# Where the output head pairs turn the next head pair, and where they take the left-over queries

## The chip, the cores and the metric

The kernel runs on one core of one Trainium2 chip. The metric is the device time of one execution in microseconds; before the change it is 324.42 us, the median of 3 runs (324.22 to 324.81). A core has a tensor engine for matrix products (TensorE; PE in the profile, PEld for its weight loads), a vector engine (DVE), a scalar engine (ACT), GpSimd (POOL) and a queue engine (SP). Each works through its own list of instructions and waits on semaphores for the others. TensorE writes into PSUM, eight banks of 128 x 512 fp32, from which DVE and ACT read.

## The reference

Attention with a relative position bias, followed by a feed-forward layer whose hidden units are the largest of three products:

```
scores = q @ k^T / sqrt(64) + bias[|i - j|]       # 8 batches, 8 heads, 576 positions, head size 64
attn   = softmax(scores)
x      = (attn @ v), heads side by side           # 4608 tokens x 512
h      = max(x @ w1, x @ w2, x @ w3)              # 4608 x 768
out    = h @ w_out                                # 4608 x 512
```

## The kernel before

Work goes by head pairs: batch `b` and pair `hp`, four pairs to a batch, 32 in all. The 576 positions are four tiles of 128 and a remainder of 64, "left-over" keys and queries. A head pair does these things:

- The queries and keys of the pair are turned by `turn` (L782): 28 small transposes on TensorE (tile `tp`, one buffer of the score pool) and five copies on DVE into `qT`, `kT` and `xT`. `turn(n)`, called in pair `n`, turns the queries and keys of pair `n + 1` and the attention output of pair `n - 2`.
- Scores for one key tile (`key_scores`, L877) are two matmuls and one exponential on ACT into `e4`; the bias is applied afterwards by DVE, as a product with exponentials of the bias (`times_band`, L826, and its kin). Left-over keys (`left_keys_rows`, L906, tile `sct`) and left-over queries (`left_queries`, L934, tile `scq`; then `times_band_left`, L941) go into `el` in the same way.
- Attention times values (`attend_rows`, L994, tile `a`) comes one head pair later: it is the first thing that a pair does for the pair before it, after which DVE divides by the sums.

Between these, each head pair carries one stage of the feed-forward layer of the batch before, handed out as a queue of `stages` (L393 to 666). Three stages of four are gate stages: two feature blocks of `hT` each, for which TensorE computes the first and second product in the pair and the third in the next pair (`after`, L541), and DVE takes the largest. The last maximum is `larger` (L549, instruction L551); in the code it is the callback `largest`. The fourth stage is the output stage (`outputs`, L621): four products of 128 tokens with `w_out`, of which the first two form one tile `ps0` and the third and fourth one tile each by halves (`halves`, L581). Head pairs that carry it are the *output head pairs*: (3,1), (4,1), (5,1), (6,1) and (7,1), five in all. The diff touches the gate stage's `run` too, but only in its list of arguments and one call.

A product over 128 rows is split in two halves of 64 rows that run side by side on TensorE, with a `rows(False)` part and a `rows(True)` part (`pair`, L370). In the output stage `rows0(False, c0, c1)` works on feature blocks `c0` to `c1 - 1`: blocks 0 to 3 were finished in earlier pairs, blocks 4 and 5 are written by the two instructions of `largest` in this same head pair. `begin1` is the first part of the third product, `end0` the second part of `ps0` with the ACT copy of its first half into `osb`; `put` is the DVE copy of its other half, and `end1` the second part and the DVE copy of the third product.

PSUM is full. The score pool `ps_s` has two buffers (of two banks), through which `sc`, `sct`, `tp` and `scq` rotate in the order of their creation; `ps_a` has one buffer, used by `ps0` and `a` in turn; `ps_f` has one, used by the third gate product and the output products by halves.

Order is written out by hand. TensorE's matmuls (`mm`, L108) and transposes (`tr`, L112), DVE's instructions (`dve_copy`, L125, and the rest), ACT's copies and, in this part of the kernel, its exponentials are all kept in program order on their engine; so are the DMA issues on their queues. An instruction that has to wait holds up everything behind it on its engine. The order within an output head pair is the body of `run` (L638), called from the main loop at L1294:

Of the kernel before, what the change touches and what calls it, by code (L numbers as in the profile page):

```python
# [39 lines left out]
def kernel(  # L40
# [19 lines left out]
    HP = H // 2  # L60
# [309 lines left out]
    def pair(n, operands, pool, tag, w=CH):  # L370


        box = []

        def rows(swap, c0=0, c1=n):
            if not swap and c0 == 0:
                box.append(pool().tile([P, 2, CH], F32, tag=tag, name="psp"))
            made = []
            for c in range(c0, c1):
                for par in range(2):  # L380
                    i = par ^ swap
                    lhsT, rhs = operands[i](slice(64 * par, 64 * par + 64), c)
                    made.append(mm(
                        box[0][:, i, 0:w], lhsT=lhsT, rhs=rhs, start=not swap and c == 0, stop=swap and c == n - 1,
                    ))
            if swap:
                behind_rows(made[0], box[1])
            elif c1 == n:
                box.append(first_rows_end())

        return lambda: box[0][:, :, 0:w], rows

    def ffn(t0, nt, last, tiled=False):  # L393
# [124 lines left out]
        def gates(fb, m):  # L518

            def gate(i, ki):  # L520
                return lambda r, c: (
                    w_bf[ki][r, c, (fb + i) * P : (fb + i) * P + P], xT[r, c, t0 : t0 + nt]
                )

            ps0, rows0 = pair(DCH, (gate(0, 0), gate(1, 0)), lambda: ps_a, "a")
            ps1, rows1 = pair(DCH, (gate(0, 1), gate(1, 1)), lambda: ps_f, "ff")

            def end0():
                rows0(True)
                m.append(ffnw.tile([P, 2, CH], BF16, tag="m", name="m"))  # L530
                for i in range(2):
                    st[fb + i]["m"] = m[0][:, i, :]
                act_copy(m[0][:], ps0())

            def end1():
                rows1(True)
                return lambda: inorder(nc.vector.tensor_tensor(  # L537
                    out=m[0][:], in0=ps1(), in1=m[0][:], op=ALU.max,
                ))

            def after():  # L541
                ps2, rows2 = pair(DCH, (gate(0, 2), gate(1, 2)), lambda: ps_f, "ff")

                def end(parts=1):
                    rows2(True)
                    out_ = hT[:, fb * CH : fb * CH + 2 * CH].rearrange("p (i t) -> p i t", i=2)
                    n = 2 // parts

                    def larger():  # L549
                        for i in range(0, 2, n):  # L550
                            inorder(nc.vector.tensor_tensor(  # L551
                                out=out_[:, i : i + n], in0=ps2()[:, i : i + n], in1=m[0][:, i : i + n], op=ALU.max,
                            ))
                    return larger
                return lambda: rows2(False), end

            def run(more_scores, left, ahead, largest, bands, keys):
                rows0(False)
                largest()
                more_scores()  # L560
                bands()
                end0()
                rows1(False)
                left()
                ahead()
                end1()()

            run.keys_late = False
            return run, after

        def columns(j, c0, c1):
# [49 lines left out]
        def outputs():  # L621
            ps0, rows0 = pair(FCH, [columns(j, 0, d_model) for j in range(2)], lambda: ps_a, "a")

            def end0():
                rows0(True)
                osb = osb_tile()
                first = act_copy(osb[:], ps0()[:, 0, :])
                put_later(0, osb)

                def put():  # L630
                    osb = osb_tile()
                    other_banks([dve_copy(osb[:], ps0()[:, 1, :])], [first])
                    put_later(1, osb)
                return put

            begin1, end1 = halves(2)

            def run(more_scores, left, ahead, largest, bands, keys):  # L638
                end_keys = keys()
                rows0(False, 0, 1)  # L640
                end_keys()
                rows0(False, 1, KT)
                largest()
                more_scores()
                bands()
                rows0(False, KT)
                begin1()
                put = end0()
                left()
                ahead()  # L650
                put()
                end1()()

            run.keys_late = True
            return run, lambda: halves(3)
# [221 lines left out]
    def key_scores(qT, kT, e4, t):  # L877
        sc = ps_s.tile([P, 2, QM], F32, tag="sc", name="sc")
        for par in range(2):
            r = slice(64 * par, 64 * par + 64)  # L880
            mm(sc[:, par, :], lhsT=kT[r, P * t : P * t + P], rhs=qT[r, 0:QM])
        exp(e4[:, t], sc[:])
# [230 lines left out]
    for hp in range(HP):  # L1113
        qT, kT = (x[:, hp, :] for x in qk[0])
        e4, el = e_tiles()
# [29 lines left out]
    for hp in range(HP):  # L1145
        qT, kT = (x[:, hp, :] for x in qk[0])
        if begun:
            e4, el = begun.pop()
            more_transposes(hp + 1)
            scores(qT, kT, e4, 1, 2)  # L1150
        else:
            e4, el = e_tiles()
# [58 lines left out]
    for b, hp in [(b, hp) for b in range(1, B) for hp in range(HP)]:  # L1211
        if hp == 0:
            x_sb[b] = x_tile()
        qT, kT = (x[:, hp, :] for x in qk[b])
        e4, el = begun[0] if begun else e_tiles()
# [13 lines left out]
        if tiled:  # L1229
            run, after = stages.pop(0)  # L1230
# [37 lines left out]
        if rows:  # L1268
            begin2, end2 = thirds.pop()()
            if not run.keys_late:  # L1270
                end_keys = left_keys_rows(qT, kT, el)
            begin2()
            if not run.keys_late:
                end_keys()
            if not lead:
                key_scores(qT, kT, e4, 2)
            largest = end2(2 if run.keys_late else 1)

            def bands():
                times_band(hp, e4, 2, 0, QM, inorder)  # L1280
                times_bandt(hp, el)
                times_band(hp, e4, 3, 0, QM, inorder)

            def left():
                left_queries(hp, qT, kT, el)
                times_band_left(hp, el)

            def ahead():
                n = HP * b + hp + 1
                if n < HP * B:  # L1290
                    begun.append(e_tiles())
                    key_scores(*(x[:, n % HP, :] for x in qk[n // HP]), begun[0][0], 0)

            run(  # L1294
                lambda: (turn(HP * b + hp), key_scores(qT, kT, e4, 3)), left, ahead, largest, bands,
                lambda: left_keys_rows(qT, kT, el),
            )
            thirds.append(after)
        elif tiled:
            if len(pending) > 1:  # L1300
                fill(DCH)
            keys()
            fill(FCH)
            times_band(hp, e4, 0, 0, QS, inorder)
            begin0, end0, begin1, end1, alone = run
            scores(qT, kT, e4, *order[2])
            begin0()
            exp_left = left_queries(hp, qT, kT, el)
            turned_1 = begin1()
            if (b, hp) == (3, 0):  # L1310
                left_keys(hp, qT, kT, el, 0, S)
            times_band(hp, e4, 1, 0, QM, inorder)
            band_left = times_bandt(hp, el)
            go_behind([band_left], turned_1[-1])
            times_band_left(hp, el)
            scores(qT, kT, e4, *order[3])
            dve0 = end0([exp_left])
            dve1 = end1([band_left])
            times_band(hp, e4, 2, 0, QM, inorder)
            dve0()  # L1320
            times_band(hp, e4, 3, 0, QM, inorder)
            dve1()
            pending.extend((n, [fn]) for n, fn in alone)
        else:
            fill(8 if (b, hp) == (2, 1) else rate, keys, *([lambda: None] if together else []))
            if b == 1 and hp + 1 < HP:
                spread_packed(hp + 1, nc.vector)
            times_bandt(hp, el)


            def beside_scores():
                banks = [pool.tile([P, KT * 64], F32, tag=tag, name="scq") for pool, tag in ((ps_a, "a"), (ps_f, "ff"))]
                turn_left_queries(qT, kT, banks)
                put_left_queries(el, banks)

            visit(qT, kT, e4, order[2:], None if together else beside_scores, el=el if together else None)
# [100 lines left out]
```

## Time and profile before

| what | value |
|---|---|
| median of 3 runs | 324.42 us (324.22 to 324.81) |
| the profiled execution's own time | 324.71 us |
| its span, first to last instruction | 322.9 us |
| granted TensorE clock, mean | 0.998 |
| TensorE busy | 306.3 us, 95% of the span |
| DVE busy | 235.9 us, 73% |
| ACT busy | 200.8 us, 62% |
| POOL busy | 143.4 us, 44% |
| `psp` products 64x512, count | 800 matmuls, 99.4 us busy |

Times of single instructions are from this one execution. Where two instructions follow each other on one engine, the second can start shortly before the first is shown to end, so sums go from start to start. A line such as L109, L113 or L126 is that of a helper that records all matmuls, transposes or copies; tiles tell them apart. The ends of matmuls are modelled. In lists of waits, a wait for several semaphores is put down to the one that came last.

### The profile page before, as it was taken

The numbers are of one execution on the slowest core, as the hardware profiler recorded it, in microseconds if no ns is written. First come the engines' busy times: TensorE is split into PE (matmuls) and PEld (weight loads), VectorE is DVE, ScalarE is ACT, GpSimd is POOL, SyncE is SP. The second block draws the span as 40 slices with busy tenths as digits, with TensorE's granted clock in tenths as the row PEclk, the third lists the DMA queues.
The fourth block names the chain that finished last, engine by engine and source line by source line (L and its number), as shares of the span: only waits on it lengthen the run. The fifth ranks groups of instructions, "written<-read, shape, count | busy, mean of one in ns | idle before, by whom it ended". The sixth has DMA issues, their size and how long they took to land.

```text
span 322.9 us, 12536 instructions
## 1 busy us (share of the span) xinstructions
PE 306.3 (95%) x5539; PEld 197.5 (61%) x5539; DVE 235.9 (73%) x576; ACT 200.8 (62%) x268; POOL 143.4 (44%) x199
## 2 busy tenths in 40 slices
PE   7789999999999899989999899989998999999995
PEld 2357877764666676657666666666666664444442
DVE  7489897878788688877887788868886775454452
ACT  4989988775776577757775677657775741121221
POOL 8989788497968273844576275800000000000000
PEclk9999999999999999999999999999999999999999
DMA  9999999999979776995999497941002000301103
GB/s 162 206 181 198 178 103 86 145 75 190 121 48 100 133 80 43 88 89 120 65 63 81 138 79 50 87 108 37 2 2 103 35 2 3 130 0 65 67 0 131
DMA packets 117430, 29.00 MB, mean 90 GB/s; under 512 B 106232, under 2 KB 112896, under 8 KB 117376
## 3 DMA queue, kind: packets, MB, share of 16 engines
q0 software_dynamic: 105664, 16.66, 70.1%
q1 hardware_dynamic: 9952, 11.08, 9.9%
q8 instruction: 43, 0.70, 0.9%
q10 hardware_dynamic: 1760, 0.47, 0.6%
q14 instruction: 11, 0.09, 0.1%
HBM read 35.39 MB, written 9.45 MB: 139 GB/s over the span
## 4 chain that ended last, share of the span: by engine, by line
PE 81%; ACT 8%; DVE 5%; DMA 3%; issue 1%; SPq 0%; DVEq 0%; ACTq 0%
PE psp L109 34%; PE ps L109 15%; PE a L109 12%; PE sc L109 7%; PE pso L109 5%; ACT e L850 5%; PE tp L113 3%; DMA xT<-in_k_dram 2%; PE sct L109 2%; ACT el L850 2%; DVE e L830 1%; PE scq L109 1%; DVE qT L126 1%; DVE x_sb L986 1%; DMA out_dram<-osb 1%
## 5 line engine op out<-in xcount | busy, mean ns | idle before, releaser
L850 ACT ACTIVATE e<-sc 128x1024 bf16<-128x1024 f32 x128 | 129.4, 1026 | 44.0 <-PE sc L109 41.1
L109 PEld LDWEIGHTS <-w_bf 64*128 64x128 bf16 (+1 forms) x1120 | 77.8, 95 | 52.2 <-issue 0.9
L109 PE MATMUL psp<-xT,w_bf 64*128 64x512 bf16 x800 | 99.4, 376 | 0.0
L830 DVE TENSOR_TENSOR e<-e,hank 128x512 bf16<-128x512 bf16 (+2 forms) x120 | 56.5, 476 | 1.9 <-ACT e L850 1.7
L109 PE MATMUL ps<-xT,w_bf 128*128 128x512 bf16 (+1 forms) x320 | 57.2, 331 | 0.0
L109 PE MATMUL sc<-qT,kT 64*128 64x512 bf16 (+1 forms) x336 | 49.1, 327 | 3.2 <-DVE kT L126 1.2
L199 POOL DMA_DIRECT2D q_sb<-in_q_dram x48 | 36.8, 784 | 31.3 <-PE tp L113 26.8
L109 PE MATMUL a<-vx,e 64*128 64x65 bf16 (+1 forms) x1728 | 45.5, 190 | 0.1
L109 PEld LDWEIGHTS <-e 64*128 64x128 bf16 (+1 forms) x1728 | 41.0, 94 | 5.4 <-issue 0.8
L109 PEld LDWEIGHTS <-kT 64*128 64x128 bf16 (+1 forms) x700 | 29.5, 94 | 21.8 <-issue 4.9
L109 PEld LDWEIGHTS <-hT 64*128 64x128 bf16 (+1 forms) x462 | 29.8, 95 | 16.8 <-issue 0.9
L199 POOL DMA_DIRECT2D k_sb<-in_k_dram x48 | 36.6, 783 | 7.1 <-PE ps L109 4.6
L167 POOL DMA_DIRECT2D vx<-in_v_dram x28 | 25.0, 912 | 22.5 <-PE a L109 18.1
L109 PE MATMUL a<-vt,el 64*128 64x65 bf16 (+1 forms) x270 | 29.1, 197 | 5.3 <-ACT e L850 5.3
L109 PEld LDWEIGHTS <-el 64*128 64x128 bf16 (+1 forms) x702 | 26.6, 94 | 12.3 <-DVE osb L126 6.7
L850 ACT ACTIVATE el<-sct 128x576 bf16<-128x576 f32 (+2 forms) x36 | 21.7, 605 | 15.7 <-PE sct L109 14.3
L109 PE MATMUL psp<-wo_bf,hT 64*128 64x256 bf16 (+1 forms) x360 | 31.2, 305 | 0.0
L421 ACT ACTIVATE m<-ps 128x512 bf16<-128x512 f32 x14 | 8.4, 597 | 35.3 <-PE ps L109 35.3
L126 DVE COPY qT<-tp 128x512 bf16<-128x512 bf16 (+3 forms) x63 | 19.8, 319 | 9.6 <-PE tp L113 9.1
L551 DVE TENSOR_TENSOR hT<-psp,m 128x1024 bf16<-128x1024 f32 (+1 forms) x21 | 19.9, 968 | 9.0 <-PE psp L109 9.0
L537 DVE TENSOR_TENSOR m<-psp,m 128x1024 bf16<-128x1024 f32 x17 | 20.8, 1225 | 3.7 <-PE psp L109 3.6
L109 PE MATMUL pso<-wo_bf,hT 128*128 128x512 bf16 (+2 forms) x102 | 21.9, 367 | 0.4 <-DVE m L430 0.4
(83 smaller groups left out, 372.4 us busy)
## 6 DMA issues: line engine op xcount, KB each, us to landing
out_dram<-osb SPq DMA_DIRECT2D x35, 256.0 KB, 2.0
vx<-in_v_dram POOLq DMA_DIRECT2D x28, 128.0 KB, 3.9
q_sb<-in_q_dram POOLq DMA_DIRECT2D x50, 64.0 KB, 3.1
k_sb<-in_k_dram POOLq DMA_DIRECT2D x48, 64.0 KB, 3.7
w_bf<-in_moe_w_dram POOLq DMA_DIRECT2D x2, 512.0 KB, 8.1
xT<-in_k_dram SPq DMA_DIRECT2D x6, 128.0 KB, 4.8
hank<-w_dr SPq DMA_DIRECT2D x2, 384.0 KB, 5.5
w_bf<-in_moe_w_dram POOLq DMA_DIRECT2D x1, 768.0 KB, 8.3
```

The lines of the kernel that those rows point to most:

```text
L109: made = inorder(nc.tensor.matmul(*args, **kw))
L113: inorder(nc.tensor.transpose(*args))
L126: return inorder(nc.vector.tensor_copy(out_, in_))
L167: in_turn(b, nc.gpsimd.dma_start(out=dst[:, t, h0:h1, :], in_=x[:, t, h0:h1, :]), P * (h1 - h0))
L199: in_turn(b, nc.gpsimd.dma_start(out=dst[:, g, :, par, :], in_=part), KT * P)
L421: nc.scalar.activation(out=st[fb]["m0"][:], in_=ps0, func=ACTF.Copy)
L537: return lambda: inorder(nc.vector.tensor_tensor(out=m[0][:], in0=ps1(), in1=m[0][:], op=ALU.max,))
L551: inorder(nc.vector.tensor_tensor(out=out_[:, i : i + n], in0=ps2()[:, i : i + n], in1=m[0][:, i : i + n], op=ALU.max,))
L830: put(nc.vector.tensor_tensor(out=e4[:, t, :, lo:hi], in0=e4[:, t, :, lo:hi], in1=hank[:, 2 * hp : 2 * hp + 2, c0:c1][:, :, ::-1], op=ALU. ...
L850: made = nc.scalar.activation(out=out_, in_=in_, func=ACTF.Exp, scale=inv_sqrt_d)
L986: divided[b, hp, half] = inorder(nc.vector.tensor_tensor(out=x_sb[b][:, 2 * half : 2 * half + n, P * hp : P * hp + P].rearrange("p t (h d) ...
```

## The change

The call that computed `turn` and the last key tile's scores together is split in two arguments, `turn_next` and `more_scores`. In a gate stage the two are called one after the other, as before. In an output stage `turn_next` is called before the products of feature blocks 1 to 3 (and so before `largest`), `more_scores` stays where it was, and `left` (left-over queries and their product with the bias) is called before `end0` instead of after it.

```diff
@@ gates
-            def run(more_scores, left, ahead, largest, bands, keys):
+            def run(turn_next, more_scores, left, ahead, largest, bands, keys):
                 rows0(False)
                 largest()
+                turn_next()
                 more_scores()
                 bands()
                 end0()
@@ outputs
-            def run(more_scores, left, ahead, largest, bands, keys):
+            def run(turn_next, more_scores, left, ahead, largest, bands, keys):
                 end_keys = keys()
                 rows0(False, 0, 1)
                 end_keys()
+                turn_next()
                 rows0(False, 1, KT)
                 largest()
                 more_scores()
                 bands()
                 rows0(False, KT)
                 begin1()
+                left()
                 put = end0()
-                left()
                 ahead()
                 put()
                 end1()()
@@ main loop
             run(
-                lambda: (turn(HP * b + hp), key_scores(qT, kT, e4, 3)), left, ahead, largest, bands,
+                lambda: turn(HP * b + hp), lambda: key_scores(qT, kT, e4, 3), left, ahead, largest, bands,
                 lambda: left_keys_rows(qT, kT, el),
             )
```

## The prediction

> **What bounds the kernel now.** I read the page first, then the waits of the whole run, then the chain of work that ended last around one output head pair, then the timelines of the vector engine, the scalar engine and TensorE over the same stretch. The page says what kind of kernel this is:
>
> ```profile
> span 322.9 us, 12536 instructions
> ...
> PE 306.3 (95%) x5539; PEld 197.5 (61%) x5539; DVE 235.9 (73%) x576; ACT 200.8 (62%) x268; POOL 143.4 (44%) x199
> ```
>
> TensorE is busy for 95% of the span, and the others only count where they make it wait. So the price of an edit is how much TensorE idle time it adds or takes away. The waits name the one idle spot that belongs to the output head pairs (total us, times, longest us):
>
> ```profile
> DVE el L943 <- ACT el L850: 14.1, 22, 1.6
> ...
> ACT osb L123 <- PE psp L109: 6.9, 5, 1.4
> PEld L109 <- DVE osb L126: 6.7, 5, 1.3
> ```
>
> The last line occurs five times, and there are five output head pairs. To see how it arises I take the pair from 172.5 to 178.9 us; the stretches from 104.2, 138.3, 206.6 and 240.6 look alike, down to 0.02 us from the maxima (L551) to the copies of the transposes. Columns of the chain: start, duration, what.
>
> ```profile
> 173.06 0.14 PE sct L109 x2
> 173.20 0.65 PE psp L109 x6
> 173.84 0.41 PE tp L113 x28
> 174.25 0.22 PE sc L109 x2
> 174.47 2.41 PE psp L109 x28
> ...
> 176.90 0.33 ACT osb L123
> 177.24 0.16 issue
> 177.40 0.59 ACT el L850
> 177.99 0.93 ACT e L850
> ```
>
> The 28 `psp` matmuls at 174.47 are, in program order, four products of feature blocks 4 and 5 (0.43 us at the rate of the pairs above them, 0.65 us for 6), twelve of `begin1` and twelve of `end0`. At 176.88 the chain leaves TensorE. The vector engine over this stretch (start, duration, line; a merged entry runs on for several instructions):
>
> ```profile
> 172.76 1.29 DVE L551 TENSOR_TENSOR hT<-psp,m 128x512 bf16<-128x512 f32 x2 [0.41 <-PE psp L109]
> 174.29 0.42 DVE L126 COPY qT<-tp 128x512 bf16<-128x512 bf16 x1 [0.24 <-PE tp L113]
> ...
> 175.13 0.51 DVE L126 COPY xT<-tp 128x512 bf16<-128x512 bf16 x2
> 175.56 0.55 DVE L830 TENSOR_TENSOR e<-e,hank 128x768 bf16<-128x768 bf16 x1
> ...
> 178.02 0.22 DVE L943 TENSOR_TENSOR el<-el,hank 128x128 bf16<-128x128 bf16 x1 [1.41 <-ACT el L850]
> 178.16 1.28 DVE L126 COPY osb<-psp 128x512 f32<-128x512 f32 x2
> ```
>
> And what TensorE and the scalar engine do at the end:
>
> ```profile
> 178.90 0.20 PE L109 MATMUL a<-vt,el 64*128 64x65 bf16 x2 [1.06 <-ACT e L850]
> ```
>
> ```profile
> 176.90 0.60 ACT L123 ACTIVATE osb<-psp 128x512 f32<-128x512 f32 x1 [1.37 <-PE psp L109]
> 177.40 0.59 ACT L850 ACTIVATE el<-scq 128x512 bf16<-128x512 f32 x1
> ```
>
> The reader is to see a detour. The second half of the first output product ends at 176.88, and `ps_a` (one buffer) must be emptied before the next pair's attention product, which writes there. The scalar engine empties its half at 176.90. The vector engine could empty the other half at once, but its copy (`put`) is queued behind `times_band_left` (L943), which waits for the exponentials of the left-over queries, which sit behind the scalar copy. So that copy starts at 178.16, takes 0.68 us (the median of that group) and ends at 178.84; attention starts 0.06 us later. The trace names the exponential `e` as the releaser, since it ends at the same moment; the weight loads name the copy, and the attention product does not read that `e`. TensorE would have been done with `end1` at 177.88 (176.88 + 0.12 `scq` + 0.22 `sc` + 0.66 for twelve 256-column products, each a row of the chain in a neighbouring pair). The stall is 178.90 - 177.88 = **1.02 us per pair, five times**.
>
> **The change part by part.** It acts in the five output head pairs only; in the gate pairs `turn_next` and `more_scores` are called in the order that they had.
>
> *Left-over queries ahead of `end0`.* Eight `scq` matmuls (0.12 us) move ahead of `end0`; TensorE's sum is the same. Their exponential then runs while `end0` computes (1.32 us: 2.41 less 0.43 and 0.66), L943 follows it, and `put` waits for `end0` alone. The 1.02 us of stall goes. What is late next: the `put` copy would be done about 0.03 + 0.68 + 0.06 = 0.77 us after `end0`, while TensorE has 0.22 + 0.66 = 0.88 us of work left there. So the cover is thin, 0.11 us, but it holds, and should it fail the cost is the shortfall alone. On the scalar engine the `osb` copy is now behind the exponential instead of ahead of it; that one is over before `end0` ends. `el`'s buffer of scores is the one that the transposes used, free since their copies. Value: **-1.02 us per pair**. Bounds: 0 if `ps_a` came free no earlier, -1.06 by the idle time that the timeline shows.
>
> *Transposes ahead of blocks 1 to 3.* TensorE does the same 28 transposes (0.41 us) after `sct` at 173.20 instead of after the six products at 173.84. Inputs are there: the batch was loaded a head pair or more ago, and their score buffer was freed by the exponential that ended at 171.88 + 1.02 = 172.90. The chain shows 0.41 us for 28 transposes in the following gate pair too, so the place is worth nothing in itself. No DMA is issued by either moved step. POOL's long waits for transposes are for the last pair of a batch, not for these; stores on SP's queue keep their order.
>
> But the moved call also takes its five copies on the vector engine ahead of `largest()`, the two maxima that write feature blocks 4 and 5 of `hT` and free `ps_f`. That engine works in the order written: L943's 1.41 us of waiting with a ready copy behind it shows that. So:
> - Transposes end at 173.20 + 0.41 = 173.61; copies start 0.04 us later (174.25 to 174.29 now), at 173.65. Until then the vector engine idles, though the maxima could have run at 172.76.
> - Copies take 1.27 us start to start (174.29 to 175.56): to 174.92.
> - Maxima: two in 1.29 us, 0.69 us each (median 0.686), so the second starts 0.60 us after the first. They end at 175.61 and 176.21.
> - TensorE: products of blocks 1 to 3 end at 173.61 + 0.65 = 174.26, scores of key tile 3 at 174.48 (its buffer, `sct`'s, is free at 173.29 + 0.65 = 173.94). Block 4 must wait for the first maximum: 175.61 + 0.06 = 175.67, a stall of 1.19 us. Its two products take 0.22 us; block 5 waits from 175.89 to 176.27, another 0.38 us. `begin1` also needs the maxima, and is covered by that.
> - Together **+1.57 us per pair**. What used to hide the maxima was the transposes and six products; now only six products and two score matmuls stand beside copies and maxima of 2.56 us.
>
> No row shows a matmul waiting for these maxima. If block 4 waited for both, it would start at 176.27 and block 5 follow 0.22 us later: +1.79. If the q copy could begin with its own transposes done, at the earliest 8 of 28, the copies would begin up to 0.29 us sooner: +1.28. I take +1.57: the two maxima are separate instructions on separate blocks, and today's copy starts only after the last transpose.
>
> Sum: after the stalls, TensorE has 2.41 + 0.12 + 0.22 + 0.66 - 0.22 = 3.19 us from block 5 to the end, 176.27 to 179.46, and attention starts there instead of at 178.90: +0.56 us per pair (1.57 - 1.02, rounded). The `ps_a` copy would be done by 179.36. The next pair's first exponential then ends at about 180.1, 0.6 us into the attention product; its next score tile comes 0.9 us after that product's start, and the copies of `end1` free `ps_f` at about 180.2, over a microsecond ahead of their need. So nothing is handed on. Five pairs: **+2.8 us**. The profiled run took 324.71 us (its span 322.9, 1.8 around it), so 327.5 there; it stood 0.29 over the median 324.42, so **327.2 us**.
>
> On the clock: the granted clock is 1.00 in this stretch, with TensorE busy for 5.34 of 6.40 us and one idle gap of 1.06. The new gaps (1.19, 0.38) are of that size, and I charge nothing beyond the idle time. The Trainium skill, "TensorE: Matmul & The Clock Gate", Part 1, speaks against leaving TensorE idle: a window of some 3.4 us counted as idle halves its clock for at least another. No run here shows an output pair throttled; by that rule, were a window counted idle, an estimate from the page is up to 1.7 us more per pair, 8.5 in all. The sum above goes by the row.
>
> **The rivals.**
> 1. *The maxima are not late* (faster). If they ran ahead of the copies after all, or their stall stayed short, the left-over queries' gain would stand alone: 324.4 - 5 x 1.02 = 319.3. The place is block 4's wait for the first maximum, the point of decision a stall of 1.02 us per pair. Against it: the order in which the vector engine's work is written, and its idling in order at 178.02.
> 2. *Both maxima are waited for at block 4*: +0.22 us per pair more, 328.3. For it: a wait is often coarser than the data; against: two instructions.
> 3. *The left-over queries win nothing*, because `ps_a` comes free late again: +1.57 x 5 = 332.3. The 0.11 us margin speaks for it, but missing the margin costs little more than what it misses.
> 4. *The copies start with the first transposes*: +0.26 us per pair, 325.7. Against it: 174.25 to 174.29.
>
> **How the numbers follow.** Forecast (326.0 to 328.0) 0.69, rival 2 0.12, rival 4 0.05, rival 3 0.05, rival 1 0.06, and 0.03 that the two terms cancel within 0.2%, about what a measurement can tell from no change. Slower: 0.91; same 0.03; faster 0.06. The range from rival 4 to a little above rival 2, 325.7 to 328.5, holds 0.86; the likeliest's own range stands in it.
>
> **What would show it.** In the profile after: the copies of `tp` start ahead of L551 in the output pairs, at about 0.9 us after the preceding end of the gate's third product; weight loads or matmuls `psp <- wo_bf,hT` wait for DVE `hT` L551 about 1.2 us, five times, and again for 0.4; the wait of the weight loads for DVE `osb` is gone; L943 runs before `end0` ends. The prediction is wrong if no wait for L551 shows, if attention still waits for `osb`, or if the stretch of an output pair is not about 0.56 us longer.

## The result, and the profile after

The changed kernel takes 327.27 us (median of 20 runs), the kernel before 324.70 us (median of 20 runs beside it): a ratio of 1.007, with a 95% interval of 1.0049 to 1.0092. It is slower by 2.6 us; 327.2 us had been forecast, within 325.7 to 328.5.

The profiled execution took 327.02 us. Its page begins:

```profile
span 325.2 us, 12526 instructions
## 1 busy us (share of the span) xinstructions
PE 308.1 (95%) x5539; PEld 196.4 (60%) x5539; DVE 236.6 (73%) x576; ACT 201.2 (62%) x268; POOL 143.6 (44%) x199
```

The engines carry out as many instructions as before, and TensorE's busy time is up by 1.8 us, that of DVE, ACT and POOL by at most 0.7; the span is 2.3 us longer. The waits of the whole run (total us, times, longest us) say why:

```profile
DVE qT L126 <- PE tp L113: 15.0, 16, 1.6
...
PEld L109 <- DVE hT L551: 10.4, 10, 1.6
...
PE psp L109 <- DVE hT L551: 6.9, 10, 1.2
...
PEld L109 <- DVE osb L126: 1.0, 5, 0.2
```

The wait of the weight loads for the copy into `osb` has shrunk from 6.7 us to 1.0. In its place, weight loads and matmuls wait ten times, twice per output pair, for the maxima (L551). The first line is the vector engine's side: it waits 15.0 us instead of 9.1 for transposes, since copies now stand at the head of its queue while maxima that could run are behind them.

The chain of work that ended last, in the output pair that now runs from 173.5 us:

```profile
174.15 0.42 PE tp L113 x28
174.57 0.02 issue
174.60 0.42 DVE qT L126
175.02 0.40 DVE kT L126
175.42 0.10 DVE qT L126
175.52 0.43 DVE xT L126 x2
175.95 1.21 DVE hT L551 x2
177.15 0.05 issue
177.20 1.04 PE psp L109 x14
178.24 0.12 PE scq L109 x8
178.36 1.29 PE psp L109 x12
179.66 0.22 PE sc L109 x2
179.87 0.66 PE psp L109 x12
180.53 0.84 PE a L109 x50
```

Before, this chain ran through TensorE from `sct` to the end of `end0` and left it only then. Now it leaves TensorE after the transposes, goes through all five copies and both maxima, and returns at 177.20. From there to the attention product it stays on TensorE: the detour at the end is gone. TensorE's and the vector engine's own rows:

```profile
175.03 0.40 PE L109 MATMUL sc<-qT,kT 64*128 64x512 bf16 x2
176.60 0.39 PE L109 MATMUL psp<-wo_bf,hT 64*128 64x512 bf16 x2 [1.18 <-DVE hT L551]
177.20 1.04 PE L109 MATMUL psp<-wo_bf,hT 64*128 64x512 bf16 x14 [0.21 <-DVE hT L551]
178.08 0.28 PE L109 MATMUL scq<-qT,kT 64*128 64x64 bf16 x8
...
180.44 0.20 PE L109 MATMUL a<-vt,el 64*128 64x65 bf16 x2
```

```profile
174.60 0.42 DVE L126 COPY qT<-tp 128x512 bf16<-128x512 bf16 x1 [1.30 <-PE tp L113]
...
175.86 1.28 DVE L551 TENSOR_TENSOR hT<-psp,m 128x512 bf16<-128x512 f32 x2
...
179.03 0.23 DVE L945 TENSOR_TENSOR el<-el,hank 128x128 bf16<-128x128 bf16 x1 [0.92 <-ACT el L852]
179.69 0.69 DVE L126 COPY osb<-psp 128x512 f32<-128x512 f32 x1 [0.43 <-PE psp L109]
```

Block 4 waits for the first maximum, block 5 for the second. `times_band_left` (now L945) is over before `end0` ends, and `put` starts the moment `end0` has ended.

To compare pairs without mixing engines I take the start of the exponential of the left-over keys (`el <- sct`) in one output pair and in the next, four head pairs later. In the kernel before, and in the changed one:

```profile
173.29 0.65 ACT L850 ACTIVATE el<-sct 128x576 bf16<-128x576 f32 x1 [0.40 <-PE sct L109]
...
207.35 0.65 ACT L850 ACTIVATE el<-sct 128x576 bf16<-128x576 f32 x1 [0.39 <-PE sct L109]
```

```profile
174.25 0.65 ACT L852 ACTIVATE el<-sct 128x576 bf16<-128x576 f32 x1 [0.39 <-PE sct L109]
...
208.88 0.65 ACT L852 ACTIVATE el<-sct 128x576 bf16<-128x576 f32 x1 [0.39 <-PE sct L109]
```

That is 34.06 us before and 34.63 after: **+0.57 us per output pair**. I call this distance the period. Of its four intervals, the one that begins in the output pair grows from 8.37 to 8.88 us and the next from 7.98 to 8.05; the last two keep their 8.19 and 9.52 us. The first two periods before are less even (34.39 and 33.97, with one gate pair of 9.80 us ahead of the second output pair); over all four the mean is +0.53.

### The profile page after: what moved, and what is told of

Its sections match the earlier page's. It is cut to its first block, busy times and chain, and to the rows that moved or that the text cites. A ratio compares the mean times of both kernels' runs of the same rounds, so it can differ in the third digit from the quotient of the medians.

```text
span 325.2 us, 12526 instructions
## 1 busy us (share of the span) xinstructions
PE 308.1 (95%) x5539; PEld 196.4 (60%) x5539; DVE 236.6 (73%) x576; ACT 201.2 (62%) x268; POOL 143.6 (44%) x199
## 4 chain that ended last, share of the span: by engine, by line
PE 81%; DVE 10%; ACT 6%; issue 1%; DMA 1%; ACTq 0%; DVEq 0%
PE psp L109 34%; PE ps L109 15%; PE a L109 12%; PE sc L109 7%; PE pso L109 5%; ACT e L852 4%; PE tp L113 3%; PE sct L109 2%; DVE hT L551 2%; DVE qT L126 2%; DVE e L832 1%; PE warm L109 1%; DVE kT L126 1%; DVE xT L126 1%; ACT el L852 1%
## 5 line engine op out<-in xcount | busy, mean ns | idle before, releaser
L109 PEld LDWEIGHTS <-hT 64*128 64x128 bf16 (+1 forms) x462 | 27.3, 95 | 27.3 <-DVE hT L551 10.4
L109 PE MATMUL psp<-wo_bf,hT 64*128 64x256 bf16 (+1 forms) x360 | 32.8, 305 | 6.9 <-DVE hT L551 6.9
L852 ACT ACTIVATE el<-scq 128x512 bf16<-128x512 f32 (+1 forms) x38 | 19.5, 530 | 10.5 <-PE scq L109 10.5
L551 DVE TENSOR_TENSOR hT<-psp,m 128x1024 bf16<-128x1024 f32 (+1 forms) x21 | 19.9, 966 | 6.9 <-PE psp L109 6.9
```

The costliest lines, as they stand in the source:

```text
L109: made = inorder(nc.tensor.matmul(*args, **kw))
L551: inorder(nc.vector.tensor_tensor(out=out_[:, i : i + n], in0=ps2()[:, i : i + n], in1=m[0][:, i : i + n], op=ALU.max,))
L852: made = nc.scalar.activation(out=out_, in_=in_, func=ACTF.Exp, scale=inv_sqrt_d)
```

## The experiments

My theory: two separate effects in each output pair, a stall at the maxima because the copies go ahead of them on the vector engine, and a detour to the attention product that the early left-over queries remove. The rivals: that the left-over queries win nothing, that the place of the transposes on TensorE is what costs, that TensorE waits for both maxima at once. All diffs are against the changed kernel, in the `run` of the output stage unless said otherwise.

**Left-over queries alone.**

```diff
                 end_keys()
-                turn_next()
                 rows0(False, 1, KT)
                 largest()
+                turn_next()
                 more_scores()
```

> Only the left-over queries go ahead of end0; the transposes are called where they were before the change. Theory (the left-over queries end a detour worth 1.02 us per output pair, the early transposes cost 1.57): about 324.6 - 5.1 = 319.5 us, ratio to before 0.984, and the wait of the weight loads for DVE osb (6.7 us in five) falls to about 1 us or less. Rival, the left-over queries win nothing: about 324.6, ratio 1.000.

Measured: 320.14 us, ratio 0.9859 (0.9837 to 0.9880). The wait for `osb` falls to 0.9 us, and the rival is out. The gain is 4.5 us instead of 5.1; the period is 33.08 us, 0.98 below the kernel before. It would be more but for a gap that the theory did not have. In the chain of this run, and in the rows of three engines:

```profile
172.04 1.09 PE psp L109 x16
173.12 0.03 issue
173.15 0.29 PE scq L109 x8
```

```profile
172.07 1.02 ACT L852 ACTIVATE e<-sc 128x1024 bf16<-128x1024 f32 x1 [0.56 <-PE sc L109]
...
172.70 0.51 DVE L126 COPY xT<-tp 128x512 bf16<-128x512 bf16 x2
...
173.15 0.29 PE L109 MATMUL scq<-qT,kT 64*128 64x64 bf16 x8
```

The gap of 0.03 us and the 0.29 us of the eight `scq` matmuls are together 0.20 more than the 0.12 that these take in the chain of the changed kernel. In TensorE's row they start 1.29 us after the first of the 16 matmuls ahead of them (171.86), which need 1.09. Two candidates end just here. The vector engine copies `xT` out of the transposes' tile until 173.21, but the left-over scores start 0.06 us before that, in all five output pairs, so they do not wait for it. The exponential of key tile 3's scores ends at 173.09, 0.06 us before they start, and in the trace the first `scq` matmul waits on the semaphore that the scalar engine's instructions raise. The pool has two buffers, so in this order of calls the left-over scores must take over that of key tile 3's scores and not that of the transposes; the buffers are not handed on strictly in the order of creation, as my description of the kernel has it. The expectations of the two runs below that move the left-over queries further take the copies for the cause of the 0.20 us.

**Transposes alone.**

```diff
                 begin1()
-                left()
                 put = end0()
+                left()
                 ahead()
```

> Only the transposes go ahead of blocks 1 to 3; the left-over queries stay behind end0. Theory: the stall at the maxima with nothing to set against it, 5 x 1.57 = 7.9 us, about 332.4 us, ratio 1.024; the wait for DVE osb is still there, about 6.7 us. Rival, the left-over queries win nothing and the transposes cost only the net change: about 327.2, ratio 1.008.

Measured: 333.81 us, ratio 1.0282 (1.0255 to 1.0310). The period is 35.79 us, +1.73. Both costs are in TensorE's rows, the stalls at the maxima and the old detour:

```profile
179.00 0.39 PE L109 MATMUL psp<-wo_bf,hT 64*128 64x512 bf16 x2 [1.18 <-DVE hT L551]
179.60 2.34 PE L109 MATMUL psp<-wo_bf,hT 64*128 64x512 bf16 x26 [0.21 <-DVE hT L551]
...
184.01 0.20 PE L109 MATMUL a<-vt,el 64*128 64x65 bf16 x2 [1.08 <-ACT e L852]
```

So the two effects are separate, and the larger one was sized too small: +1.73 per pair, not 1.57.

**Both moves, the maxima first.**

```diff
                 end_keys()
+                largest()
                 turn_next()
                 rows0(False, 1, KT)
-                largest()
                 more_scores()
```

> Both moves of the change, but the two maxima (largest) are issued ahead of the transposes' copies. Transposes are as early on TensorE as in the changed kernel. Theory (the order on the vector engine is the cause): no wait for L551, about 319.5 us, ratio 0.984, as with the left-over queries alone. Rival (the place of the transposes on TensorE, or their score buffer, is the cause): 327.2, ratio 1.008, as the changed kernel.

Measured: 318.33 us, ratio 0.9802 (0.9781 to 0.9823); on another chip, beside the last three experiments, 318.12 us, ratio 0.9797 (0.9784 to 0.9809). Transposes are as early on TensorE as in the changed kernel; only their copies and the maxima have changed places on the vector engine. The wait for L551 is gone, and with it 9 us. That settles the cause. The period is 32.88 us: -1.18 against before, and 1.75 below the changed kernel, the same stall that the transposes alone showed. Without it TensorE goes from the scores of key tile 3 to the left-over queries in 1.31 us, where the changed kernel took 3.05 (175.03 to 178.08):

```profile
171.35 0.40 PE L109 MATMUL sc<-qT,kT 64*128 64x512 bf16 x2
171.57 1.27 PE L109 MATMUL psp<-wo_bf,hT 64*128 64x512 bf16 x16
172.66 0.30 PE L109 MATMUL scq<-qT,kT 64*128 64x64 bf16 x8
```

This kernel is the best of both: 6.3 to 6.6 us below the kernel before.

**One maximum first.** `larger` gets a range, so that the maximum of block 4 can be called by itself.

```diff
-                    def larger():
-                        for i in range(0, 2, n):
+                    def larger(i0=0, i1=2):
+                        for i in range(i0, i1, n):
...
                 end_keys()
+                largest(0, 1)
                 turn_next()
                 rows0(False, 1, KT)
-                largest()
+                largest(1, 2)
```

> Both moves, with the maximum of block 4 ahead of the transposes' copies and that of block 5 behind them. Theory: block 4 does not wait, block 5 waits until the end of copies and one maximum, 173.65 + 1.27 + 0.69 + 0.06 = 175.67 against 174.70 without a wait: a stall of 0.97 us per pair in place of 1.57, so 5 x (0.97 - 1.02) = -0.3 us against before, about 324.3, ratio 0.999. If only the first wait mattered: 319.5. If TensorE waits for both at once wherever they stand: 327.2 or more.

Measured: 324.01 us, ratio 0.9985 (0.9969 to 1.0001); period 34.03 us, -0.03 against before. Block 4 starts unhindered, block 5 waits:

```profile
173.93 0.40 PE L109 MATMUL psp<-wo_bf,hT 64*128 64x512 bf16 x2
175.29 1.04 PE L109 MATMUL psp<-wo_bf,hT 64*128 64x512 bf16 x14 [0.96 <-DVE hT L551]
```

Each block waits for its own maximum. That TensorE waits for both wherever they stand is refuted, and with one of the two maxima in front about a third of the loss comes back (0.60 of 1.75 us per pair).

**Left-over queries yet earlier.** On the kernel with the maxima first:

```diff
                 rows0(False, KT)
+                left()
                 begin1()
-                left()
                 put = end0()
```

> Both moves with the maxima first, and the left-over queries yet 0.66 us earlier, ahead of begin1. Theory (the left-over scores wait for the buffer that the transposes' copies still read, which is what costs 0.20 us per pair when the left-over queries are moved alone): they would start at 172.00 in that run's frame, the copies end at about 172.58, so 0.6 us of stall per pair, 3.0 us in all, about 321.3 us. Rival (those 0.20 us come from something else, such as a fetch of instructions): no new stall, about 318.3.

Measured: 321.43 us, ratio 0.9895 (0.9882 to 0.9908); period 33.54 us, 0.66 above the kernel with the maxima first. Now the profile names the wait:

```profile
173.10 1.02 ACT L852 ACTIVATE e<-sc 128x1024 bf16<-128x1024 f32 x1 [0.56 <-PE sc L109]
...
173.39 0.51 DVE L126 COPY xT<-tp 128x512 bf16<-128x512 bf16 x2
...
173.96 0.29 PE L109 MATMUL scq<-qT,kT 64*128 64x64 bf16 x8 [0.46 <-DVE xT L126]
```

With the maxima first the left-over scores do take over the transposes' buffer: they start 0.06 us after the copies end (173.90) and 0.16 before the exponential of key tile 3 is over (174.12). So the 3.0 us came as forecast, but the run says nothing of the 0.20 us in the other order, where the wait is for the exponential.

**Left-over queries yet later.** On the kernel with the left-over queries alone; `end0` gets a start, `rows0(True, c0)`:

```diff
                 begin1()
+                rows0(True, 0, 2)
                 left()
-                put = end0()
+                put = end0(2)
```

> The left-over queries alone are moved, but behind the first four of the twelve matmuls of end0 (0.43 us later); transposes late as before the change. Theory of the buffer: the copies are over by then, the 0.20 us per pair go, 1.0 us below the left-over queries moved alone: about 319.1, and 8.04 and 7.14 us between the exponentials of the left-over keys as with the maxima first. Rival: no difference to the left-over queries moved alone, 320.1 and 7.34 us.

Measured: 319.01 us, ratio 0.9829 (0.9805 to 0.9853). The period is 32.89 us, against 33.08 with the left-over queries right behind `begin1`, and 7.14 us pass from the exponential in the output pair to the next. So the 0.20 us are gone. The run cannot tell whose wait they were: copies (until 173.65) and exponential (until 173.54) are both over when the left-over scores start at 173.82. That it was the exponential rests on the rows of the run with the left-over queries alone. The medians, 319.01 and 320.14, come from different chips and scatter by up to 2.9 us; the periods are what shows the gain. The period is also that of the kernel with the maxima first (32.88): early transposes by themselves win nothing.

**More cover for the copy that empties `ps_a`.** On the kernel with the maxima first; `begin1` takes a range of blocks:

```diff
-                begin1()
+                begin1(0, 4)
+                rows0(True, 0, 2)
                 left()
-                put = end0()
+                put = end0(2)
+                begin1(4)
                 ahead()
```

> Maxima first, and four of the twelve matmuls of begin1 go behind end0, so that 1.10 us of TensorE work instead of 0.88 stand beside the copy that empties ps_a; the left-over queries stay at about the same time, behind four matmuls of end0. Theory: the last 0.07 us per pair between the end of end1 and the attention product go, 0.35 us: about 318.0. Rival (that gap is TensorE's own start, not the copy): 318.3.

Measured: 318.29 us, ratio 0.9804 (0.9785 to 0.9822), no different from the 318.12 us beside it. The time alone would fit the rival, 318.3. In the profile the effect is there: no wait for `osb` is left, attention follows at once, and the period is 32.83 us instead of 32.88.

```profile
177.17 0.83 PE L109 MATMUL psp<-wo_bf,hT 64*128 64x256 bf16 x12
177.82 0.21 PE L109 MATMUL a<-vt,el 64*128 64x65 bf16 x2
```

Twelve 256-column matmuls, 0.65 us from start to start, and no gap. So that gap was the copy, about 0.05 us per pair; 0.3 us in all is less than these times resolve.

## Why the prediction was right

The forecast was right in its sign, its cause and its size, but the two terms of the sum were each sized about 0.2 us too small, and these errors cancel.

- *The order on the vector engine.* Right, almost to the hundredth. Against the start of `sct` in the chain (172.72 before, 173.67 after), copies were to start 0.93 us later and do (174.60); block 4 was to start 2.95 us later and does so at 2.93 (176.60), block 5 at 3.55 and does at 3.53 (177.20). The stall was taken from durations of the profile before and from nothing else.
- *The size of that stall.* "Together +1.57 us per pair" was too small: 1.73 with the transposes alone, 1.75 between the changed kernel and the one with the maxima first. The failing step is the point in time at which TensorE would have gone on: 174.48 was read from the chain, which counts a matmul to its end. In a running stream the next matmul has started 0.18 us before that: the row for the 28 products before the change says 174.29, where the chain says 174.47. A wait moves the start, so 0.17 to 0.18 us more belongs to it.
- *The size of the gain.* "1.02 us per pair" fails in the same way. `end1` was taken to end at 177.88; by starts it makes room for attention at 177.00 + 0.66 = 177.66, and 178.90 - 177.66 = 1.24. Of these, 1.18 came with the maxima first and 1.23 with more cover.
- *The difference.* 1.75 - 1.18 = 0.57 per pair, 0.56 forecast: the two omissions cancel. That is not luck alone, since both come from the same reading of ends for starts, and the prediction also added the net up in one go: block 5 starts within 0.02 us of the forecast, and from there to the attention product it is 3.24 us (177.20 to 180.44) instead of 3.19. Five times 0.57 is 2.9 us; the medians differ by 2.6.
- *"The cover is thin, 0.11 us, but it holds."* It did not quite, and a wait for `osb` was among the signs of being wrong. It was to be gone and is 1.0 us on the weight loads in five; on TensorE about 0.05 us per pair, by the experiment with more cover. The margin reached to the end of `end1` in the chain (180.53), but attention could have started at 179.71 + 0.66 = 180.37.
- *The score buffer of the left-over queries, "free since their copies".* Nothing contradicts it for the change: the copies end at 175.94, 2.1 us before the left-over scores start. For the left-over queries alone it names the wrong tile: there they wait for the exponential of key tile 3 and lose 0.20 us per pair. I had not worked out the buffers' times for any order but the changed one.
- *Nothing handed on.* Right but for 0.07 us: from the exponential of the pair behind an output pair to the next one 8.05 us pass, 7.98 before, and later pairs keep their length.
- *The rivals.* Maxima not late: refuted, though its price, a kernel with only the gain, became the best version, and 1 us better than its 319.3. Both maxima waited for at once: refuted by two separate waits, and by the experiment with one maximum first. The left-over queries win nothing: refuted by the first experiment. Copies that start with the first transposes: refuted, 174.57 to 174.60 again.
- *The clock.* Right to charge nothing: the new gaps, 1.18 and 0.21 us in TensorE's row, leave the granted clock at 1.00 in every stretch from 33 to 300 us. The rule of the Trainium skill that was weighed against the row ("TensorE: Matmul & The Clock Gate", Part 1) needs a whole window of about 3.4 us counted as idle; these gaps did not make one.

## What to carry to other kernels

Where a step is moved on one engine, write down the order that it brings about on every other engine, and follow the queue that works strictly in that order: here 28 transposes moved by 0.65 us on TensorE cost 1.75 us, because five copies went ahead of two maxima on the vector engine, and calling the maxima first made the same move harmless. To size a stall, subtract a start from a start: in these profiles, where the ends of matmuls are modelled, the end of a matmul in a stream lies about 0.18 us behind the point at which the next could begin. And when an operation goes earlier, ask whose buffer it takes over and when that was last read, and check the answer against the rows: a copy that ends close by need not be what was waited for.

## What the runs showed of the hardware

Executions of one kernel can differ by 3 us and more; the 20 of the kernel before lie between 324.18 and 327.49. In one case the trace shows a cause far from the change. The profiled execution of the kernel with more cover took 320.78 us where the median is 318.29. Its row of TensorE at 24 us, and its stretches of 2 us around it (length, then busy time and instructions of PE, PEld, DVE, ACT and POOL, granted clock, DMA share, GB/s):

```profile
23.98 0.37 PE L113 MATMUL xp<-ident,x_sb 128*128 128x128 bf16 x2 [1.89 <-DVE qT L126]
```

```profile
22.00:24.00 2.00, 0.11 (x8) 0.11 (x2) 2.00 (x4) 0.84 (x3) 1.49 (x2) 0.93 1.48 188
24.00:26.00 2.00, 2.00 (x25) 1.50 (x25) 1.93 (x8) 0.38 (x1) 1.61 (x2) 0.50 1.73 183
26.00:28.00 2.00, 2.00 (x35) 1.38 (x35) 1.67 (x5) 1.96 (x2) 1.96 (x4) 0.71 1.27 207
```

TensorE waited 1.89 us for a copy of the vector engine, and the clock granted to it then stood at 0.50 from 23.73 to 27.14 us, 3.41 us long. The kernel with the maxima first, on the same chip, has neither the gap nor the drop, and in the output pairs, far behind it, the clock is 1.00 in both. No other kept trace has a gap of over 1.2 us on TensorE, nor a lower clock from 33 us to the last 2 us of its span; the run with the transposes alone has, in the output pair shown, gaps of 1.18, 0.21 and 1.08 us within 6.2 us and stays at 1.00. A half clock for 3.4 us fits the rule of the Trainium skill ("TensorE: Matmul & The Clock Gate", Part 1). How much idle time it takes was not tested here, and why the copy came late in this execution stays open.
